# A fused spectral filter and feed-forward kernel: another order of work in its first 50 microseconds

## The chip, the cores and the metric

The kernel runs on one core of one Trainium2 chip. The metric is the time of one execution on the device, in microseconds (us); the time of a kernel is the median of its runs.

A core has five engines that run side by side, each through its own instructions in order: TensorE (PE in the profile, its weight loads PEld) multiplies matrices into PSUM, VectorE (DVE) and ScalarE (ACT) do elementwise work, GpSimd (POOL) does small work here, SyncE (SP) issues DMAs. An instruction waits at the head of its engine's queue until what it needs is there, and everything behind it on that engine waits too.

## What is computed

```python
xn = layernorm(x)                               # x: 2048 rows (tokens) of 1024
s  = irfft2(rfft2(xn) * (w_r + 1j * w_i))       # spectral filter over both axes
g  = silu(silu(xn @ w1) @ w2)                   # w1: 1024 x 3584, w2: 3584 x 1024
return x + s * g
```

## The kernel before, in words

The rows are cut into four **row blocks** c = 0 to 3 of 512 rows, each of four **row tiles** p of 128 rows. w1 is cut into 28 **weight tiles** f of 128 columns. All large products run with f16 operands that are split into a high and a low part; a product of a row block and a weight tile, `mm1(c, f)` (L449), is 24 matmuls of 128 x 512: eight slices of the inner dimension, by (high, high), (high weight, low row) and (low weight, high row).

**A row tile** is prepared in `ln_gen` (L679): `load_x` issues its DMA (L641), `stats` takes its statistics on VectorE (L685 to L688) and three small operations on GpSimd, `norm` normalises on ScalarE (L693), `trans` turns it with eight transposes on TensorE (L702), `hi` copies the high part out of PSUM on ScalarE (L706), `lo` makes the low part on VectorE (L710). Two PSUM buffers serve these transposes and the first stage of the forward transform (`fa_mat`, L762, its matmuls at L766 to L768). Blocks 2 and 3 go another way, `turned` (L650): normalised and copied on ScalarE (L693 and L671), low part on VectorE (L664), then turned by DMA (L657). Their normalised tiles have two buffers, so the third waits for the first one's low part.

**A weight tile** is prepared in `weights1` (L261): `load` issues its DMA (L271), `maxi` takes each row's largest magnitude on VectorE (L274), `scales(i, k)` sums that over the partitions with a small matmul on TensorE (L258) for k tiles together and makes a power of two and its inverse in four to six short VectorE operations (L279 to L287), `split` writes the high part on ScalarE (L251) and `rest` the low part on VectorE (L254). Raw and split tiles share seven buffers.

**The order of the work** is written out by hand: what the program emits is what each engine executes in order. Background work stands in generators, each a job in a queue: `wq` for w1 and later w2, `bg` for row blocks and then the spectral transforms, `xq` for a scan of w2. `slot(queue)` runs the first job on to its next `yield`. The main loop (L1467) goes through `order`, a list of pairs (c, f): first (0, 0) to (0, 3), then (1, 0) to (1, 3), (0, 4), (0, 5), (1, 4), (1, 5), then block 2. Here the products are called by their place n in that list, the first, the fifth and so on (n = 0, n = 4). After each product from n = 4 on, `after` (L1409) evicts the product before it (ScalarE, L465; where a pair of blocks and tiles is complete, also subtractions and splits for the second matrix product, L494 to L499 and L251/L254), and `work` (L1415) gives `wq` one slot and `bg` up to three, as many as a small reckoning of VectorE's and TensorE's work allows. At the n in `EXTRA` `wq` has a second slot. Where a block begins, `finish(bg, ln[c])` (L1470) first runs its job to the end; since that steps the queue until the job reports its end, it also takes the first step of the next job.

Before, the beginning (L1436 to L1459) loads row tiles 0 to 3, then weight tiles 0 to 3; it runs 35 idle matmuls (`spin`, L1428) and then ten slots of `bg` and `wq` in turn, with 8 or 12 idle matmuls after four of them. Weight tiles 0 and 1 are scaled together, then 2 and 3. The first product runs its 24 matmuls by kind of part, the others by slice. For n < 4 each product is followed by one slot of `wq` and 2, 0, 1 and 1 slots of `bg` (L1503): these carry block 1's preparation, the loads of weight tiles 4 and 5 and the reduce of tile 4.

Of the kernel before, what the change touches and what calls it, by code (L numbers as in the profile page):

```python
# [127 lines left out]
def spectral_ffn(ctx, tc, x, w_r, w_i, w1, w2, ca, kc, ci, tw, pm, out):  # L128
    nc = tc.nc
# [112 lines left out]


    xnT, w1t, h32, w2t = {}, {}, {}, {}
    e1, m1, r1, rs, s1 = (small(k, NFT) for k in ("e1", "m1", "r1", "rs1", "s1"))
    ep, hs = small("ep", NP), small("hs", NP)
    w2m = small("w2m", NFT)
# [13 lines left out]
    def weights1():  # L261
# [35 lines left out]
            w1t[i] = w = new.pop(i)  # L297
            low(w[:, 1], raw.pop(i), rs[:, i:i + 1], w[:, 0])

        for i in range(4):  # L300
            load(i)
        yield 0
        maxi(0)
        yield 0
        maxi(1)
        yield 0
        scales(0, 2)
        yield 0
        split(0)
        yield 0  # L310
        rest(0)
        yield 0
        split(1)
        rest(1)
        maxi(2)
        maxi(3)
        yield 0
        scales(2, 2)
        split(2)
        rest(2)  # L320
        yield 2
        split(3)
        rest(3)
        yield 2
        def ahead(i):

            if i < NFT and i not in raw and i - len(used1) <= 4:
# [118 lines left out]

    done2, ready2, chunks = [0], [-1], [0]

    def mm1(c, f):  # L449
        ps = pf.tile([128, 512], F32, name=f"pa{c}_{f}", tag="ff")  # L450
        w, xt = w1t[f], xnT[c]
        terms = [(d, wh, xh) for wh, xh in ((0, 0), (0, 1), (1, 0)) for d in range(8)]
        if c + f:
            terms.sort(key=lambda k: k[0])
        for n, (d, wh, xh) in enumerate(terms):
            nc.tensor.matmul(ps, w[:, wh, d], xt[:, xh, d], start=(n == 0), stop=(n == 23))  # L456
        if c == 3:
            used1.add(f)
        q, g = f // 2, c // 2

        def evac():
            if (q, g) not in h32:
                h32[q, g] = H["p"].tile([128, 4, 512], F32, name=f"h32_{q}_{g}", tag="h32", bufs=2)
            hq = h32[q, g]
            nc.scalar.activation(hq[:, 2 * (c % 2) + f % 2], ps, AF.Silu, scale=s1[:, f:f + 1])  # L465
            if c % 2 and f % 2:
                return hidden(q, g)

        return evac
# [209 lines left out]
    def ln_gen(c):  # L679
# [30 lines left out]
            nc.vector.tensor_tensor(xnT[c][:, 1, :, sl], pst.pop(p), xnT[c][:, 0, :, sl], op=OP.subtract)  # L710

        new_xnT(c)
        if c == 0:
            for p in range(2):
                stats(p)
                norm[p]()
            trans(0)
            hi(0)
            stats(2)
            norm[2]()  # L720
            trans(1)
            hi(1)
            stats(3)
            norm[3]()
            lo(0)
            yield 0
            trans(2)
            hi(2)
            lo(1)
            yield 0  # L730
            trans(3)
            hi(3)
            lo(2)
            yield 0
            lo(3)
            yield 0
            return
        if c in TURNED:
            yield from turned(c, stats, norm)
            return  # L740
        for i in range(4):
            pair = range(2 * (i % 2), 2 * (i % 2) + 2)
            for p in pair:
                if i < 2:
                    stats(p)
                else:
                    trans(p)
                    if c < 3:
                        load_x(c + 1, p)
            if i < 2:  # L750
                yield 2.5
                for p in pair:
                    norm[p]()
                continue
            for fn in (hi, lo):
                for p in pair:
                    fn(p)
            yield 2.5

    psa, l0 = {}, {}  # L760

# [625 lines left out]
    with tc.manual_schedule():  # L1387
# [48 lines left out]
        nc.scalar.activation(warm, ones[:, 0:1], AF.Silu)  # L1436
        J = {}
        open_fwd()
        for i in range(2):
            load_x(0, i)  # L1440
        nc.sync.dma_start(ident, pm[:, 3])
        for i in range(2, 4):
            load_x(0, i)
        w1j = add(wq, weights1())
        slot(wq)
        ln = [add(bg, ln_gen(0)), None, None, None]
        nc.gpsimd.memset(mhalf, -0.5)
        spin(WARM[0])
        for k, q in enumerate((bg, wq, bg, wq, bg, wq, wq, bg, wq, wq)):
            slot(q)  # L1450
            spin(WARM[1 + k])
        for i in range(4):
            load_x(1, i)
            if i == 1:
                load_fwd()
        for c in range(1, 4):
            ln[c] = add(bg, ln_gen(c))
        for c in range(4):
            add(bg, fd_gen(c))  # L1459

# [1 line left out]
        order += [(2, 0), (2, 1), (2, 2), (3, 0), (3, 1), (2, 3), (3, 2), (3, 3), (2, 4), (2, 5), (3, 4), (3, 5)]  # L1462
        order += [(c, f + i) for f in range(6, NFT - LAST, 2) for c in range(4) for i in range(2)]
        order += [(2 * g + c, f + i) for g in range(2) for f in range(NFT - LAST, NFT, 2) for c in range(2) for i in range(2)]
        last_use = {c: max(n for n, k in enumerate(order) if k[0] == c) for c in range(4)}
        left, f_job = len(order), None
        for n, (c, f) in enumerate(order):  # L1467
            left -= 1
            if f == 0 and c:
                finish(bg, ln[c])  # L1470
            if ln[3].done and n >= 22 and not f_job:
                add(xq, wmax_gen())
                max_job = add(xq, w2max_gen())
                f_job = add(bg, switch(A, open_f, 1, max_job))
                add(bg, f_gen())
                add(bg, edge_gen())
                add(bg, switch(B, open_i, 6, lag=2))
                for k in IORDER:
                    add(bg, i_gen(k))
            if left == 2 * LAST + 3:  # L1480
                finish(wq, w1j)
                finish(xq, max_job)
                finish(bg, f_job)
                w2_scales()
                add(wq, w2_gen())
            chunks[0] = sum(last_use[k] < n for k in range(4))
            if left == 3:
                load_h(0, 0, 0, nc.sync)
                load_h(0, 0, 1, nc.sync)
                load_h(0, 1, 0, nc.sync)  # L1490
            if left == 1:
                load_h(0, 1, 1, nc.sync)
            hold[0] = left < 4
            while f not in w1t:
                slot(wq)
            if (c, f) in FILL:
                fa_mat(0, FILL.index((c, f)))
                fa_evac(0, FILL.index((c, f)))
            ev = mm1(c, f)
            if left == 0:  # L1500
                for j, k in ((2, 0), (2, 1), (3, 0)):
                    load_h(0, j, k, nc.sync)
            if n < 4:  # L1503
                slot(wq)
                for _ in range((2, 0, 1, 1)[f]):
                    slot(bg)
                settle()
                fresh_ev[0] = ev
                tick()
                continue  # L1510
# [80 lines left out]
```

## Time and profile before

| | before |
|---|---|
| median of 3 runs | 1243.97 us (1243.03 to 1247.36) |
| profiled execution | 1243.22 us |
| its span, first to last instruction | 1241.4 us |
| TensorE busy | 1222.8 us, 98% |
| VectorE busy | 998.9 us, 80% |
| ScalarE busy | 467.6 us, 38% |
| GpSimd busy | 116.0 us, 9% |

The profile is of one execution. Its busy times are sums over the whole span, and a busy TensorE includes the idle matmuls. The timeline gives each instruction's start and duration from the span's start; where equal instructions follow each other they are merged, with their count. The waits give, for an engine and line, whom it waited for. The granted clock is the share of TensorE's full clock that the chip granted in a stretch.

### The profile page before, as it was taken

The numbers are of one execution on the slowest core, as the hardware profiler recorded it, in microseconds if no ns is written. First come the engines' busy times: TensorE is split into PE (matmuls) and PEld (weight loads), VectorE is DVE, ScalarE is ACT, GpSimd is POOL, SyncE is SP. The second block draws the span as 40 slices with busy tenths as digits, with TensorE's granted clock in tenths as the row PEclk, the third lists the DMA queues.
The fourth block names the chain that finished last, engine by engine and source line by source line (L and its number), as shares of the span: only waits on it lengthen the run. The fifth ranks groups of instructions, "written<-read, shape, count | busy, mean of one in ns | idle before, by whom it ended". The sixth has DMA issues, their size and how long they took to land.

```text
span 1241.4 us, 19019 instructions
## 1 busy us (share of the span) xinstructions
PE 1222.8 (98%) x6991; PEld 626.4 (50%) x6991; DVE 998.9 (80%) x1968; ACT 467.6 (38%) x612; POOL 116.0 (9%) x241
## 2 busy tenths in 40 slices
PE   8999999999999999999999999999999998999997
PEld 5545445444544454445445555544555553555544
DVE  7687988899788898886969899794377785796785
ACT  4865344334554565435433221122132221342211
POOL 1330000001000000010001121114111110000000
PEclk9999999999999999999999999999999999999999
DMA  7487476646668897769899999997989999696897
GB/s 249 135 173 184 134 227 204 186 141 174 207 186 244 271 280 240 221 186 268 187 290 237 304 253 209 273 256 225 270 210 306 261 350 351 227 366 213 267 351 280
DMA packets 272542, 297.87 MB, mean 240 GB/s; under 512 B 40256, under 2 KB 198720, under 8 KB 272064
## 3 DMA queue, kind: packets, MB, share of 16 engines
q1 hardware_dynamic: 252576, 237.85, 65.6%
q10 hardware_dynamic: 15840, 51.45, 12.2%
q0 software_dynamic: 4032, 7.34, 3.4%
q8 instruction: 55, 0.90, 0.3%
q14 instruction: 39, 0.32, 0.1%
HBM read 188.05 MB, written 104.35 MB: 236 GB/s over the span
## 4 chain that ended last, share of the span: by engine, by line
PE 84%; DMA 7%; DVE 6%; ACT 1%; issue 1%; SPq 1%; ACTq 0%; DVEq 0%; POOLq 0%
PE pa L456 46%; PE pb L536 10%; PE pb L535 10%; PE pb L534 10%; PE fx L938 2%; DMA sd<-s 2%; DMA out_dram<-pl 1%; DMA kk<-in_kc_dram 1%; PE iu L1189 1%; PE id L1271 1%; DMA fx<-in_A_x_dram 1%; PE fx L940 1%; PE fx L939 1%; DMA fs<-sd 1%; DMA jr<-in_B_w_dram 1%
## 5 line engine op out<-in xcount | busy, mean ns | idle before, releaser
L456 PE MATMUL pa<-xnT,w 128*128 128x512 f16 x2688 | 585.2, 379 | 1.1 <-ACT w L251 0.7
L456 PEld LDWEIGHTS <-w 128*128 128x128 f16 x2688 | 261.9, 98 | 311.9 <-DVE w L254 1.3
L534 PE MATMUL pb<-w,ht 128*128 128x512 f16 (+1 forms) x798 | 299.5, 375 | 0.0
L536 PE MATMUL pb<-w,ht 128*128 128x512 f16 (+1 forms) x798 | 299.5, 375 | 0.0
L535 PE MATMUL pb<-w,ht 128*128 128x512 f16 (+1 forms) x798 | 299.5, 375 | 0.0
L536 PEld LDWEIGHTS <-ht 128*128 128x128 f16 x798 | 78.1, 98 | 91.1
L534 PEld LDWEIGHTS <-ht 128*128 128x128 f16 x798 | 78.1, 98 | 87.0
L535 PEld LDWEIGHTS <-ht 128*128 128x128 f16 x798 | 78.1, 98 | 87.1
L465 ACT ACTIVATE h<-pa,s 128x512 f32<-128x512 f32 x112 | 75.6, 678 | 120.5 <-PE pa L456 108.6
L251 ACT ACTIVATE w<-jr,sc 128x512 f16<-128x512 f32 x98 | 68.3, 714 | 91.1 <-DMA jr<-in_B_w_dram 37.2
L254 DVE SCALAR_TENSOR_TENSOR w<-jr,sc,w 128x512 f16<-128x512 f32 x98 | 71.2, 744 | 8.1 <-ACT w L251 8.1
L254 DVE SCALAR_TENSOR_TENSOR hoone<-h,hs,hoone 128x2048 f16<-128x2048 f32 x28 | 65.7, 2346 | 8.4 <-ACT hoone L251 8.4
L251 ACT ACTIVATE hoone<-h,hs 128x2048 f16<-128x2048 f32 x28 | 56.0, 1998 | 37.9 <-DVE h L499 26.2
L251 ACT ACTIVATE hosum<-hr,hs 128x1536 f16<-128x1536 f32 x28 | 44.1, 1574 | 66.5 <-DVE hr L495 27.9
L965 ACT ACTIVATE zq<-Z,zs 128x1024 f16<-128x1024 f32 x16 | 18.4, 1149 | 98.5 <-DVE Z L1039 53.8
L254 DVE SCALAR_TENSOR_TENSOR hosum<-hr,hs,hosum 128x1536 f16<-128x1536 f32 x28 | 50.7, 1812 | 3.7 <-DMA hd_one<-hoone 2.6
L494 DVE TENSOR_TENSOR hr<-h 128x1024 f32<-128x1024 f32 x28 | 34.2, 1221 | 23.9 <-ACT h L465 23.8
L251 ACT ACTIVATE w<-w1r,rs 128x1024 f16<-128x1024 f32 x28 | 32.0, 1145 | 46.7 <-DVE w L254 31.8
L274 DVE TENSOR_REDUCE m<-w1r 128x1 f32<-128x1024 f32 x28 | 33.8, 1211 | 16.9 <-DMA w1r<-in_B_w_dram 16.9
L938 PE MATMUL fx<-vq,kq 128*128 128x256 f16 x192 | 43.2, 272 | 0.0
L939 PE MATMUL fx<-vq,kq 128*128 128x128 f16 x192 | 42.0, 219 | 0.0
L940 PE MATMUL fx<-vq,kq 128*128 128x128 f16 x192 | 42.0, 219 | 0.0
(210 smaller groups left out, 1502.9 us busy)
## 6 DMA issues: line engine op xcount, KB each, us to landing
w1r<-in_B_w_dram SPq DMA_DIRECT2D x28, 512.0 KB, 6.4
hd_sum<-hosum SPq DMA_DIRECT2D x56, 256.0 KB, 2.9
hd_one<-hoone SPq DMA_DIRECT2D x56, 256.0 KB, 3.6
hd_dif<-hoone SPq DMA_DIRECT2D x56, 256.0 KB, 3.2
w2m<-in_B_w_dram SPq DMA_DIRECT2D x28, 512.0 KB, 5.1
ht<-hd_dif ACTq DMA_DIRECT2D x32, 448.0 KB, 6.2
jr<-in_B_w_dram SPq DMA_DIRECT2D x56, 256.0 KB, 6.9
ht<-hd_sum ACTq DMA_DIRECT2D x32, 448.0 KB, 6.6
```

Source lines behind the costliest of these rows:

```text
L251: nc.scalar.activation(hi, raw, AF.Copy, scale=scale)
L254: nc.vector.scalar_tensor_tensor(lo, raw, scale, hi, op0=OP.mult, op1=OP.subtract)
L274: nc.vector.tensor_reduce(m1[:, i:i + 1], raw[i], axis=AX.XY, op=OP.max, apply_absolute_value=True)
L456: nc.tensor.matmul(ps, w[:, wh, d], xt[:, xh, d], start=(n == 0), stop=(n == 23))
L465: nc.scalar.activation(hq[:, 2 * (c % 2) + f % 2], ps, AF.Silu, scale=s1[:, f:f + 1])
L494: tt(sums[:, 0:2], hq[:, 0::2], hq[:, 1::2], op=OP.subtract)
L534: nc.tensor.matmul(ps, hh[:, 0], w[:, 0], start=first, stop=False)
L535: nc.tensor.matmul(ps, hh[:, 0], w[:, 1], start=False, stop=False)
L536: nc.tensor.matmul(ps, hh[:, 1], w[:, 0], start=False, stop=last)
L938: nc.tensor.matmul(o, k[:, c, kh, 1], v[:, c, vh], start=(n == 0), stop=False)
L939: nc.tensor.matmul(ps[:, c, 0], k[:, c, kh, 2], v[:, c, vh, 128:256], start=False, stop=False)
L940: nc.tensor.matmul(ps[:, c, 1], k[:, c, kh, 0], v[:, c, vh, 0:128], start=False, stop=(n == 2))
```

## The change

The beginning is written out anew, up to and with the first four products.

- Loads: row tiles 0 and 1, weight tile 0, row tiles 2 and 3, weight tiles 1 to 3. Block 1's four tiles are loaded inside the first product, the constants of the forward transform (L638) after it, weight tiles 4 and 5 after the third.
- Of the idle matmuls only the first 35 stay.
- Every one of the first four weight tiles is scaled alone. Tile 0's reduce and column sum come ahead of the first transposes. Tile 1's scale stands inside the first product, tile 2's inside the second, tile 3's inside the third.
- The first product runs in twelve pieces of eight matmuls, each for a quarter of the rows (128 columns) and one kind of part, in an order by row tile; row tiles 2 and 3 are transposed between pieces. Products 2 to 4 run by kind of part, in three pieces of eight 512-wide matmuls, with evictions and other work between the pieces.
- Block 1's tiles are prepared around products 2 to 4: statistics of tile 0 in product 2, of tile 1 in product 3 behind the scale and split of weight tile 3; the transposes of tiles 0 and 1 before product 4, those of tiles 2 and 3 after it.
- The main loop starts at n = 4. `wq` then stands before the reduce of weight tile 4, and `bg` at the first step of block 2. The check at a block's beginning is left out for block 1.

The core of the diff:

```diff
-WARM = [35, 8, 0, 8, 0, 8, 12, 0, 0, 0, 0]
+WARM = 35
...
-    def mm1(c, f):
+    def mm1(c, f, piece=None):
...
+        if piece:
+            for n, (wh, xh, cols) in enumerate(piece):
+                if callable(wh):
+                    wh()
+                    continue
+                for d in range(8):
+                    nc.tensor.matmul(
+                        ps[:, cols], w[:, wh, d], xt[:, xh, d, cols], start=(n + d == 0), stop=(n == len(piece) - 1 and d == 7),
+                        skip_group_check=True)
...
+        load_x(0, 0)
+        load_x(0, 1)
+        nc.sync.dma_start(ident, pm[:, 3])
+        W["load"](0)
+        load_x(0, 2)
+        load_x(0, 3)
+        for i in range(1, 4):
+            W["load"](i)
         nc.gpsimd.memset(mhalf, -0.5)
...
+        spin(WARM)
+        stats(0)
+        stats(1)
+        norm[0]()
+        norm[1]()
+        W["maxi"](0)
+        W["scales"](0, 1)
+        trans(0)
+        trans(1)
+        stats(2)
+        hi(0)
+        W["split"](0)
+        hi(1)
+        norm[2]()
+        lo(0)
+        stats(3)
+        W["rest"](0)
+        lo(1)
+        norm[3]()
+        W["maxi"](1)
...
+        def third():
+            trans(2)
+            hi(2)
+            for i in range(2):
+                load_x(1, i)
+
+        def fourth():
+            trans(3)
+            hi(3)
+            lo(2)
+            load_x(1, 2)
+            load_x(1, 3)
+
+        def second_scale():
+            W["scales"](1, 1)
+            W["split"](1)
+            lo(3)
+            W["rest"](1)
+            W["maxi"](2)
+
+        ev = mm1(0, 0, [
+            (0, 0, cols[0]), (0, 1, cols[0]), (0, 0, cols[1]), act(third), (1, 0, cols[0]), (1, 0, cols[1]), (0, 1, cols[1]),
+            act(fourth), (0, 0, cols[2]), (1, 0, cols[2]), act(second_scale), (0, 0, cols[3]), (1, 0, cols[3]), (0, 1, cols[2]), (0, 1, cols[3])])
+        load_fwd()
...
+        evs.append(mm1(0, 1, [
+            (0, 0, whole), act(settled), scale_of(2), act(lambda: W["maxi"](3), lambda: stats1(0)), (0, 1, whole), (1, 0, whole)]))
+
+        def begin():
+            stats1(1)
+            norm1[0]()
+            norm1[1]()
+
+        evs.append(mm1(0, 2, [(0, 0, whole), act(settled), scale_of(3), act(begin), (0, 1, whole), (1, 0, whole)]))
+        for i in range(4, 6):
+            W["load"](i)
+        trans1(0)
+        hi1(0)
+        stats1(2)
+        stats1(3)
+        trans1(1)
+        hi1(1)
+        lo1(0)
+
+        def rest_of():
+            norm1[2]()
+            norm1[3]()
+            lo1(1)
+
+        evs.append(mm1(0, 3, [(0, 0, whole), act(settled), act(rest_of), (0, 1, whole), (1, 0, whole)]))
+        for i in range(2, 4):
+            trans1(i)
+            hi1(i)
+            load_x(2, i - 2)
+        settled()
+        lo1(2)
+        lo1(3)
+        for i in range(2, 4):
+            load_x(2, i)
...
         for n, (c, f) in enumerate(order):
             left -= 1
-            if f == 0 and c:
+            if n < 4:
+                continue
+            if f == 0 and c > 1:
                 finish(bg, ln[c])
```

`settled` evicts the product before; `scale_of(i)` is the scale, the split and the low part of weight tile i; `cols` are the quarters and `whole` all 512 columns; `stats1`, `norm1`, `trans1`, `hi1` and `lo1` are block 1's.

More of the change, by code (lines that the diff above doesn't have):

```diff
@@ L298, in rest @@
             low(w[:, 1], raw.pop(i), rs[:, i:i + 1], w[:, 0])
-        for i in range(4):
-            load(i)
+        W.update(load=load, maxi=maxi, scales=scales, split=split, rest=rest)
         yield 0
[L303 to L324, printed above, removed]
         def ahead(i):
@@ L740, in ln_gen @@
             return
[L741 to L758, printed above, removed]
+        N[c] = (stats, norm, trans, hi, lo)
     psa, l0 = {}, {}
@@ L1438, in spectral_ffn @@
         open_fwd()
[L1439 to L1443, printed above, removed]
         w1j = add(wq, weights1())
         slot(wq)
[L1446 to L1455, printed above, removed]
@@ new lines, in spectral_ffn, with act, run @@
+        stats(1)
[16 more added lines that the diff above has]
+        W["maxi"](1)
+        cols = [slice(128 * i, 128 * i + 128) for i in range(4)]
+        whole = slice(0, 512)
+        def act(*fns):
+            def run():
+                for fn in fns:
+                    fn()
+            return run, None, None
@@ new lines, in spectral_ffn, with scale_of, run, settled @@
+        load_fwd()
+        def scale_of(i):
+            def run():
+                W["scales"](i, 1)
+                W["split"](i)
+                W["rest"](i)
+            return act(run)
+        evs = [ev]
+        def settled():
+            evs.pop(0)()
+        evs.append(mm1(0, 1, [
[4 more added lines that the diff above has]
+            norm1[1]()
@@ L1458, in spectral_ffn @@
+        settled()
[3 more added lines that the diff above has]
+            load_x(2, i)
+        ln = [None, None] + [add(bg, ln_gen(c)) for c in range(2, 4)]
         for c in range(4):
```

48 lines of the change are left out of this document (8 added, 40 removed).

## The prediction

> **What bounds the kernel now.** I read the page first, then the waits of TensorE, then the timeline of the first 75 us engine by engine.
>
> ```profile
> span 1241.4 us, 19019 instructions
> ```
>
> ```profile
> PE iu L1189 <- DVE zt L1167: 4.4, 1, 4.4
> PE tp L702 <- ACT x L693: 3.3, 3, 2.2
> PE fa L766 <- DVE xnT L710: 1.5, 1, 1.5
> ...
> PE pa L456 <- DVE w L254: 0.4, 1, 0.4
> ```
>
> The second fence (engine and line, whom it waited for, us in total, times, longest) is nearly the whole list: after its first matmul of w1, TensorE waits 1.5 us once, about 1 us once, and then not before line 1189, deep in the inverse transform. So a microsecond that TensorE gains or loses at the beginning is one of the whole time, unless that late wait takes it up. The question is when the first matmuls run, and when TensorE is free of the beginning for good.
>
> The timeline of the beginning (start, us, engine, line, tile, count; in brackets the idle time before and what ended it), one fence for each engine, first VectorE and ScalarE:
>
> ```profile
> 9.10 0.69 DVE L685 BATCH_NORM_STATS2 st<-x 128x6 f32<-128x512 f32 x1 [1.44 <-DMA x<-in_A_x_dram]
> ...
> 10.55 0.65 DVE L685 BATCH_NORM_STATS2 st<-x 128x6 f32<-128x512 f32 x1
> ...
> 13.03 1.21 DVE L274 TENSOR_REDUCE m<-w1r 128x1 f32<-128x1024 f32 x1
> 14.16 1.21 DVE L710 TENSOR_TENSOR xnT<-tp,xnT 128x1024 f16<-128x1024 f32 x1
> 15.29 1.21 DVE L274 TENSOR_REDUCE m<-w1r 128x1 f32<-128x1024 f32 x1
> ...
> 19.66 2.48 DVE L254 SCALAR_TENSOR_TENSOR w<-w1r,rs,w 128x1024 f16<-128x1024 f32 x2
> ...
> 25.19 0.16 DVE L279 TENSOR_SCALAR e<-s 128x2 int32<-128x2 int32 x1 [0.80 <-PE s L258]
> ...
> 44.48 2.36 DVE L710 TENSOR_TENSOR xnT<-tp,xnT 128x1024 f16<-128x1024 f32 x2 [2.11 <-ACT xnT L706]
> ```
>
> ```profile
> 10.12 1.02 ACT L706 ACTIVATE xnT<-tp 128x1024 f16<-128x1024 f32 x1
> 11.94 1.24 ACT L693 ACTIVATE x<-x,v 128x1024 f32<-128x1024 f32 x1 [0.79 <-POOL v L692]
> ...
> 18.48 2.19 ACT L251 ACTIVATE w<-w1r,rs 128x1024 f16<-128x1024 f32 x2 [0.77 <-DVE rs L282]
> 25.99 1.15 ACT L251 ACTIVATE w<-w1r,rs 128x1024 f16<-128x1024 f32 x1 [5.32 <-DVE rs L282]
> ```
>
> ```profile
> 0.99 5.76 PE L1433 MATMUL spin<-ones 128*128 128x256 f16 x35 [0.99 <-POOL mhalf L1447]
> 8.93 1.16 PE L702 MATMUL tp<-ident,x 128*128 128x128 f32 x8 [2.18 <-ACT x L693]
> ...
> 19.68 5.35 PE L456 MATMUL pa<-xnT,w 128*128 128x512 f16 x24 [0.71 <-ACT w L251]
> ...
> 35.37 1.94 PE L702 MATMUL tp<-ident,x 128*128 128x128 f32 x16
> ...
> 45.75 0.22 PE L766 MATMUL fa<-cas,xnT 128*128 128x128 f16 x1 [1.47 <-DVE xnT L710]
> ...
> 47.09 10.52 PE L456 MATMUL pa<-xnT,w 128*128 128x512 f16 x48
> ```
>
> ```profile
> 101.21 5.18 PE pa L456 x24
> ```
>
> The last row, of the chain, is one product of 24 matmuls: 5.18 us. The first product starts at 19.68, the fifth, of row block 1, at 47.09. That second time is the gauge of the beginning.
>
> **The change part by part.** Steps I use, each from start to start in those rows: statistics of a row tile 1.45 (9.10 to 10.55), reduce 1.13 (13.03 to 14.16), low part of a row tile 1.13 (14.16 to 15.29), low part of a weight tile 1.2 (2.48 for two), statistics to normalising 2.84 (9.10 to 11.94), transposes 0.97 (1.94 for two tiles), transposes to the high copy 1.19 (8.93 to 10.12), reduce to the scale's first operation 0.80 (the idle time at 25.19), from there to the split on ScalarE 0.80 (25.19 to 25.99), split to low part 1.18 (18.48 to 19.66).
>
> *The first tile.* It now takes the third place in SP's queue, which landed at 9.10. Bounds are 9.1 and 10.5 (the fourth place was in use at 10.55); I take 9.6, near the first, since the bytes ahead are the same and this tile's rows are shorter. The two row tiles behind it land by 13.0 at the latest, where the reduce of a tile in the fifth place began. The first is wanted at 12.4, so that may cost 0.6 at worst; the second is wanted at 16. Reduce from 9.6 to 10.8, scale begun 11.6, split possible 12.4. But the column sum now stands ahead of the first transposes on TensorE, which were possible at 8.93: they start at about 11.6. At full clock the high copy would begin at 12.8.
>
> *The clock.* Thirty-six idle matmuls go, so TensorE has nothing from 6.75 until the column sum near 11.2, over 4 us. The trace has one such gap:
>
> ```profile
> 1054.33 6.65 PE L1189 MATMUL iu<-kk,zt 128*128 128x129 f16 x72 [4.42 <-DVE zt L1167]
> ```
>
> ```profile
> 1056.00:1058.00 2.00, 2.00 (x22) 2.00 (x20) 0.16 (x1) 0.60 (x1) 0.00 (x0) 0.50 1.03 380
> ```
>
> After 4.42 us of idling the granted clock (third figure from the end) is 0.50. So I let the eight transposes take twice 0.97: high copy at 13.8, its end and the low part on VectorE at 14.85. Bounds: 1.0 less, or about 1 more if the second eight count too.
> [...]
>
> *The first product in quarters.* 96 matmuls of 128 columns do what 24 of 512 did; I cost that at nothing, since line 766's matmuls of 128 columns also keep pace (24 between 45.75 and 47.09, 1.34 us, so 5.4 for 96). It starts at 14.7 + 1.2 = 15.9, almost 4 us sooner. What then paces it is VectorE, without a gap from 14.85: low part, statistics 15.98, rest of tile 0 17.43, low part 18.63, reduce of tile 1 19.76, low part 20.89. The fourth row tile is normalised from 15.98 + 2.84 = 18.82 to 20.06, its transposes run to 21.3, two pieces of 0.45 to 22.2, then the sum of tile 1, whose scale begins on VectorE at 22.7.
>
> *Scales one at a time.* Four scalings of one tile replace two of two tiles, each with its reduce, its 0.80 there and 0.80 on, and each now inside the work that VectorE is late with: low part 23.6 (after 0.9 of scale), rest 1 24.73, reduce 2 25.93 to 27.1, scale 27.9, split 28.7, rest 2 29.88, reduce 3 31.08, statistics of block 1's first tile 32.21, scale 33.66, split 34.46, rest 3 35.64, statistics of its second tile 36.84, normalised 39.68 to 40.92. VectorE idles 0.8 + 1.1 + 1.1 in this, and before it 1.9 for the first tile (idle since 9.10 - 1.44).
>
> *What waits.* Both transposes of block 1's first tiles stand ahead of the fourth product on TensorE's queue. The third product is done at about 36.5; TensorE then waits some 3 us, with the fourth product behind the transposes, until 40.95. From there: transposes 0.97, product 5.18 to 47.1, transposes and high copy 1.19 to 48.3, then 1.06 to the low part and 1.27 to line 766 (in before high copy about 43.42, low part 44.48, 45.75), so 50.6, and 1.34 more: the fifth product starts at **52.0**, against 47.09. Bringing the start forward 4 us is given back and **4.9 us** are lost.
>
> *Queues one step behind.* Formerly the slots for n < 4 emitted the reduce of tile 4, and closing block 1 pulled the first statistics of block 2 ahead of the fifth product. Now both queues begin empty at n = 4. The rows of before behind it:
>
> ```profile
> 49.72 2.19 ACT L693 ACTIVATE xp<-x,v 128x1024 f32<-128x1024 f32 x1 [0.76 <-POOL v L692]
> ...
> 52.90 2.17 ACT L693 ACTIVATE xp<-x,v 128x1024 f32<-128x1024 f32 x1
> ```
>
> ```profile
> 63.63 1.23 DVE L494 TENSOR_TENSOR hr<-h 128x1024 f32<-128x1024 f32 x1 [4.96 <-ACT h L465]
> 64.77 0.68 DVE L495 TENSOR_TENSOR hr<-h 128x512 f32<-128x512 f32 x1
> 65.37 2.35 DVE L664 TENSOR_TENSOR xs<-xp,xs 128x1024 f16<-128x1024 f32 x2
> 67.64 1.28 DVE L254 SCALAR_TENSOR_TENSOR w<-w1r,rs,w 128x1024 f16<-128x1024 f32 x1
> ```
>
> ```profile
> 70.01 1.56 ACT L251 ACTIVATE hosum<-hr,hs 128x1536 f16<-128x1536 f32 x1
> 71.48 0.66 ACT L465 ACTIVATE h<-pa,s 128x512 f32<-128x512 f32 x1
> 72.05 1.99 ACT L251 ACTIVATE hoone<-h,hs 128x2048 f16<-128x2048 f32 x1
> ```
>
> ```profile
> 68.98 30.90 PE L456 MATMUL pa<-xnT,w 128*128 128x512 f16 x142 [0.44 <-DVE w L254]
> ```
>
> Call the fifth product's start T. Normalising and copying a row tile of block 2 take ScalarE 3.18 (49.72 to 52.90). Formerly two pairs ran from T + 2.6. Now they are emitted after the fifth product's eviction: eviction at T + 5.3, pairs to T + 12.2, next eviction to T + 12.9, two subtractions on VectorE 1.74 to T + 14.6. The sum of tiles 4 and 5 now stands behind the seventh product on TensorE (formerly before it): T + 15.6, scale done T + 16.9. Only then comes the first low part of block 2 (1.2), which frees the buffer that the third pair needs: pairs from T + 18.1 to T + 24.4, split of tile 4, its low part T + 25.6 to T + 26.85. So the ninth product, the first with tile 4, starts at T + 26.9 and not T + 21.9 (68.98 - 47.09); TensorE, free at T + 21.1, waits almost 6 us. The low part of tile 5 is emitted one product later, behind the subtractions of the next eviction; ScalarE does 1.56, 0.66, 1.15 (split 5), 1.99 and 0.66 from T + 25.5 to T + 31.5, VectorE 1.74 to T + 33.2 and the low part 1.28. The tenth product starts at T + 34.5 instead of T + 27.1 (68.98 + 5.18 - 47.09). **7.4 us** more. A drop of the clock in the 6 us wait is hidden behind tile 5.
>
> *At nothing:* the constants of line 638 load later, but are wanted at 50; loads of tiles 4 and 5 and of block 2 stand in SP's queue in the order in which their buffers come free, and are wanted at T or later; the evictions inside the products find ScalarE idle. If block 2's loads came late, that would add to the same ScalarE chain, up to 1 us.
>
> **Sum.** 4.9 + 7.4 = 12.3 on the profiled execution's 1243.22 (span 1241.4 and 1.8 around it; the median of the runs is 1243.97): **1255.5 us**.
>
> **Rivals.**
> *It works* (faster): TensorE never waits after its first piece. Without the clock's drop 14.7 + four products 20.7 + six sets of transposes 5.8 + three sums, each within the 0.80, 1.1 + line 766's 1.34 = 43.6, which is 3.5 before 47.09, and no new wait later: 1239.7. It decides at the transposes of block 1's second tile, which TensorE would reach at 34: the chain on VectorE must be 7 us shorter than I have it. For it: the quarters and the earlier split are real. Against: VectorE's row is full.
> *Only the early loss:* ScalarE catches up and tiles 4 and 5 come as before: 1248.1. *Only the late one:* the early part gains 2.0 (line 766's wait of 1.5 stays): 1243.2 + 5.4 = 1248.6.
> *The loss is taken up:* the wait at line 1189 hangs on a transfer that doesn't move, and its 4.4 us vanish; with the early loss alone 1243.7, no difference.
> *The clock again:* it also drops in the 3 us before block 1's second tile, and the fourth product runs at half for a while; 72 matmuls took 6.65 after the gap at 1049.9, where line 766's pace gives 4.0, so 2.6 more: 1258.1, and to 1261 with the second transposes and a late third block.
>
> **How the numbers follow.** Forecast 0.47; early loss alone 0.10; late loss alone 0.08; clock again 0.11; taken up 0.12; works 0.12. Slower by over 0.3% (3.7 us, about what a measurement can tell from no change, so beyond 1247.7) are the first four: 0.76. Same is 0.12, faster 0.12. The range leaves out only the last rival and the far end of the clock's: 1243 to 1261.
>
> **What would show it.** First w1 matmul near 15.9 (14.7 without the clock's drop); TensorE waiting about 3 us for ScalarE's normalising of block 1's second tile; the fifth product at 52; then waits of some 6 and 2 us on line 254's low parts of tiles 4 and 5, with ScalarE full between. It is wrong if VectorE gets through the first 40 us with clearly less idle time, or if ScalarE's pairs for block 2 start before the fifth product's eviction.

## The result, and the profile after

| | before | after |
|---|---|---|
| median | 1243.5 us (1240.58 to 1247.36, 6 runs) | 1262.06 us (1260.91 to 1267.49, 6 runs) |
| ratio, 95% interval | | 1.0154 [1.0136, 1.0171] |
| profiled execution | 1243.22 us | 1261.47 us |
| VectorE, ScalarE busy | 998.9, 467.6 us | 999.8, 468.2 us |

The changed kernel is 18.6 us slower. No engine has noticeably more work (VectorE 0.9 us, ScalarE 0.6 us); the first line of its page gives the span, 17.9 us longer:

```profile
span 1259.3 us, 19113 instructions
```

TensorE's waits in the changed kernel (whom it waited for, us in total, times, longest):

```profile
PE pa L442 <- ACT w L252: 4.4, 1, 4.4
PE tp L688 <- ACT x L679: 4.1, 3, 3.2
PE s L259 <- DVE m L275: 3.7, 1, 3.7
PE pa L442 <- ACT L L719: 3.1, 1, 3.1
PE iu L1133 <- DVE zt L1111: 2.6, 1, 2.6
...
PE pa L442 <- DVE w L255: 1.3, 2, 0.7
```

Lines have new numbers here: products are L437 (the first four) and L442, weight splits L252 and L255, column sum L259, transposes L688, normalising L679, ScalarE's copy of a turned tile L657, the DMA transposes L643. L1133 was L1189. Against the list of before there are new entries for the column sum, the ninth product (first line) and, later, `ACT L L719`; the longest wait for a tile's normalising (second line) is 3.2 us instead of 2.2. Where they stand, from TensorE's timeline:

```profile
10.35 0.38 PE L259 MATMUL s<-m,ones 128*128 128x1 f32 x2 [3.74 <-DVE m L275]
10.59 3.21 PE L688 MATMUL tp<-ident,x 128*128 128x128 f32 x16
14.24 1.66 PE L437 MATMUL pa<-xnT,w 128*128 128x128 f16 x24 [0.44 <-ACT w L252]
...
39.69 1.97 PE L688 MATMUL tp<-ident,x 128*128 128x128 f32 x8 [3.16 <-ACT x L679]
41.46 7.25 PE L437 MATMUL pa<-xnT,w 128*128 128x512 f16 x24
...
53.30 15.70 PE L442 MATMUL pa<-xnT,w 128*128 128x512 f16 x72
...
78.76 0.60 PE L442 MATMUL pa<-xnT,w 128*128 128x512 f16 x2 [4.44 <-ACT w L252]
80.08 6.70 PE L442 MATMUL pa<-xnT,w 128*128 128x512 f16 x24 [0.72 <-DVE w L255]
87.36 30.82 PE L442 MATMUL pa<-xnT,w 128*128 128x512 f16 x142 [0.58 <-DVE w L255]
...
124.01 0.59 PE L442 MATMUL pa<-xnT,w 128*128 128x512 f16 x1 [3.15 <-ACT L L719]
125.08 13.03 PE L442 MATMUL pa<-xnT,w 128*128 128x512 f16 x47 [0.49 <-DMA xnT<-xs]
```

Before, the sixteenth product, the first of row block 3, came straight behind other matmuls:

```profile
107.57 5.34 PE L456 MATMUL pa<-xnT,w 128*128 128x512 f16 x24
```

The differences of these starts say where the time went (for the tenth product, the start of its third matmul, the first that needs the weight tile's low part):

| start of | before | after | later by | new here |
|---|---|---|---|---|
| first product | 19.68 | 14.24 | -5.4 | |
| fifth | 47.09 | 53.30 | 6.2 | 6.2 |
| tenth | 74.16 (68.98 + 5.18) | 87.36 | 13.2 | 7.0 |
| sixteenth, second matmul | 107.8 | 125.08 | 17.3 | 4.1 |
| first matmul of L938, now L882 | 577.2 | 597.2 | 20.0 | 2.7 |
| first of L1189, now L1133 | 1054.3 | 1072.5 | 18.2 | -1.8 |

The second matmul of before's sixteenth product is taken 0.2 behind its first (5.18 over 24). The 2.7 behind it is the granted clock: 47 matmuls took 13.03 where 47 of those 0.216 make 10.1. The granted clock is the third figure from the end of the windows' rows:

```profile
36.00:40.00 4.00, 0.84 (x7) 0.65 (x7) 3.62 (x9) 1.60 (x2) 2.02 (x6) 0.81 0.39 131
40.00:44.00 4.00, 4.00 (x14) 2.28 (x13) 2.45 (x2) 2.85 (x4) 1.05 (x4) 0.50 0.30 94
44.00:48.00 4.00, 4.00 (x17) 1.72 (x16) 0.00 (x0) 1.56 (x2) 0.00 (x0) 0.84 0.10 39
...
122.00:125.00 3.00, 0.59 (x1) 0.10 (x1) 2.90 (x8) 2.38 (x4) 0.00 (x0) 0.80 1.15 255
125.00:128.00 3.00, 2.92 (x7) 1.05 (x8) 3.00 (x7) 0.00 (x0) 0.11 (x1) 0.50 0.74 210
```

Both of these waits of 3 us are followed by half the clock, the first for some 6.8 us (what is missing in the three rows, 0.19, 0.50 and 0.16 of 4 us, doubled): the fourth product took 7.25 (5.34 in before), the 47 matmuls from the sixteenth product on lost 2.7.

Why the sixteenth waits is read on ScalarE and SP. The first fence is before's normalising of block 3 and its DMA transposes (there L657), the second the same in the changed kernel (start, us, engine, line, tile, count; SPq is the DMA queue of SP):

```profile
82.54 2.16 ACT L693 ACTIVATE xp<-x,v 128x1024 f32<-128x1024 f32 x1
...
88.86 1.99 ACT L251 ACTIVATE hoone<-h,hs 128x2048 f16<-128x2048 f32 x1
...
88.04 6.51 SPq L657 DMA_TRANSPOSE xnT<-xs  x4
...
97.69 5.92 SPq L657 DMA_TRANSPOSE xnT<-xs  x4
```

```profile
99.15 2.00 ACT L252 ACTIVATE hoone<-h,hs 128x2048 f16<-128x2048 f32 x1 [5.86 <-DMA hd_one<-hoone]
...
101.63 2.17 ACT L679 ACTIVATE xp<-x,v 128x1024 f32<-128x1024 f32 x1
...
106.28 16.82 SPq L643 DMA_TRANSPOSE xnT<-xs  x8
```

In before block 3's first normalising stood ahead of the `hoone` copy, now it stands behind it, and that copy waits 5.86 us for a DMA. The normalising begins 48.3 behind the fifth product (101.63 - 53.30) instead of 35.5 (82.54 - 47.09), and the eight transposes run until 123.1. So the wait belongs to them, though its first part is booked on an eviction.

### The profile page after: what moved, and what is told of

It reads as the page before. It is cut to its first block, busy times and chain, and to the rows that moved or that the text cites. A ratio compares the mean times of both kernels' runs of the same rounds, so it can differ in the third digit from the quotient of the medians.

```text
span 1259.3 us, 19113 instructions
## 1 busy us (share of the span) xinstructions
PE 1228.5 (98%) x7031; PEld 629.1 (50%) x7031; DVE 999.8 (79%) x1976; ACT 468.2 (37%) x612; POOL 113.7 (9%) x243
## 4 chain that ended last, share of the span: by engine, by line
PE 84%; DMA 6%; DVE 5%; ACT 3%; issue 1%; SPq 1%; POOL 0%; ACTq 0%; DVEq 0%; POOLq 0%
PE pa L442 41%; PE pb L520 11%; PE pb L521 11%; PE pb L522 11%; DMA jr<-in_B_w_dram 2%; PE fx L882 2%; PE id L1215 1%; DMA pd<-pl 1%; ACT xp L679 1%; DMA out_dram<-pl 1%; PE fx L884 1%; PE fx L883 1%; PE pa L437 1%; PE iu L1133 1%; DMA fs<-sd 1%
## 5 line engine op out<-in xcount | busy, mean ns | idle before, releaser
L442 PE MATMUL pa<-xnT,w 128*128 128x512 f16 x2592 | 568.5, 381 | 9.4 <-ACT w L252 4.4
L442 PEld LDWEIGHTS <-w 128*128 128x128 f16 x2592 | 253.7, 99 | 313.3 <-issue 9.7
L252 ACT ACTIVATE w<-jr,sc 128x512 f16<-128x512 f32 x98 | 68.3, 714 | 90.1 <-DMA jr<-in_B_w_dram 28.9
L255 DVE SCALAR_TENSOR_TENSOR w<-jr,sc,w 128x512 f16<-128x512 f32 x98 | 71.2, 744 | 9.6 <-ACT w L252 9.6
L252 ACT ACTIVATE hoone<-h,hs 128x2048 f16<-128x2048 f32 x28 | 56.0, 1999 | 48.3 <-DVE h L485 20.7
L255 DVE SCALAR_TENSOR_TENSOR hoone<-h,hs,hoone 128x2048 f16<-128x2048 f32 x28 | 65.6, 2344 | 10.1 <-ACT hoone L252 10.1
L252 ACT ACTIVATE hosum<-hr,hs 128x1536 f16<-128x1536 f32 x28 | 44.1, 1574 | 65.8 <-DVE hr L481 35.2
L255 DVE SCALAR_TENSOR_TENSOR hosum<-hr,hs,hosum 128x1536 f16<-128x1536 f32 x28 | 50.7, 1811 | 1.9 <-ACT hosum L252 1.9
L252 ACT ACTIVATE w<-w1r,rs 128x1024 f16<-128x1024 f32 x28 | 32.1, 1146 | 37.2 <-DVE w L255 22.8
L882 PE MATMUL fx<-vq,kq 128*128 128x256 f16 x192 | 43.2, 273 | 0.0
```

The costliest lines, as they stand in the source:

```text
L252: nc.scalar.activation(hi, raw, AF.Copy, scale=scale)
L255: nc.vector.scalar_tensor_tensor(lo, raw, scale, hi, op0=OP.mult, op1=OP.subtract)
L882: nc.tensor.matmul(o, k[:, c, kh, 1], v[:, c, vh], start=(n == 0), stop=False)
```

## The experiments

Each time is a median of several runs, beside runs of the kernel before on the same chip. Two questions were open: which of the early and the late part costs what, and what holds block 3 back.

**One step of each queue put back.** The change, and ahead of the main loop:

```diff
+        slot(wq)
+        slot(bg)
```

> The changed kernel, with one slot of wq (the reduce of weight tile 4) and one of bg (block 2's first statistics) emitted before the fifth product, so that both queues stand there as in the kernel before. Theory (three waits, of which two come from the queues standing one step behind): the fifth product stays at about 53, the ninth and tenth come 22 and 27 us after it, the sixteenth no longer waits for block 3; 6 us slower than before, about 1249.5 us. Rival (the loss is the clock, halved because the idle matmuls are gone): the early gaps stay as they are, so most of the loss stays, 1257 to 1262. Rival (all of it is lost before the fifth product and only handed on): no change, 1262.

Measured: 1258.19 against 1242.78, ratio 1.0109 [1.0078, 1.0139]: a miss of 8.7 us. The ninth product has no wait left, as expected, but the sixteenth has:

```profile
62.44 46.78 PE L442 MATMUL pa<-xnT,w 128*128 128x512 f16 x216
...
116.69 0.58 PE L442 MATMUL pa<-xnT,w 128*128 128x512 f16 x1 [4.79 <-DMA xnT<-xs]
117.88 12.28 PE L442 MATMUL pa<-xnT,w 128*128 128x512 f16 x47 [0.60 <-DMA xnT<-xs]
```

My theory, that the two empty queues are the whole late loss, fell. The single steps show why.

**Only `wq`'s step.**

> The changed kernel with only the slot of wq (reduce of weight tile 4) ahead of the fifth product. Theory: the sum of tiles 4 and 5 comes before the seventh product again and the split of tile 4 ahead of block 2's third normalising, so the 7 us of waiting at the ninth and tenth products go; block 2 and 3 stay one step behind, so the wait at the sixteenth stays, perhaps longer since TensorE comes earlier (4 to 7 us with the clock): 1254 to 1258 us. If what counts is ScalarE's chain of block 2 and not the place of the sum, the ninth product still waits and it stays near 1262.

Measured: 1256.7, ratio 1.011 [1.008, 1.0139]. The time is as expected, the place of the remaining wait is not: the waits for tile 4 are gone, and of 5.1 us of waits for transposes 4.0 (3.46 and 0.58) stand at the thirteenth product, the first of block 2, and 1.1 at the sixteenth, where I had expected the whole.

**Only `bg`'s step.**

> The changed kernel with only the slot of bg (block 2's first statistics) ahead of the fifth product. Theory: ScalarE normalises block 2 from the fifth product on, tile 4's low part is ready before the ninth product needs it, tile 5's about 2 to 3 us late, block 3 in time for the sixteenth: 1250 to 1254 us. If the place of the sum of tiles 4 and 5 is what counts, the ninth and tenth wait as in the changed kernel, and it stays at 1256 to 1262.

Measured: 1264.32, ratio 1.0166 [1.0139, 1.0193]: a miss, no gain at all. Its ninth and sixteenth products stand where the changed kernel has them:

```profile
78.60 1.03 PE L442 MATMUL pa<-xnT,w 128*128 128x512 f16 x2 [4.43 <-ACT w L252]
...
124.08 0.38 PE L442 MATMUL pa<-xnT,w 128*128 128x512 f16 x1 [3.07 <-ACT L L719]
```

Something takes `bg`'s step back. It is the small reckoning. It books every matmul on TensorE, the idle ones too: 36 of them, 256 columns at 0.4215e-3, make 3.9 us. With these gone it stands, when the fifth product has been emitted, at 34.4 for TensorE and, with `bg`'s step put back, at 37.2 for VectorE (38.4 with both steps), and `work` gives `bg` no slot while VectorE is more than 1.0 ahead. A step put back by hand is then withheld behind the fifth product. (Without it, in the changed kernel, VectorE stands at 34.3 and `bg` has its slot: there the empty queue is enough to make block 3 late.)

**The reckoning put back as well.** Both steps, and

```diff
+        clock["pe"] += 36 * 256 * 0.4215e-3
```

> The change, with one step of wq and one of bg put back before the fifth product, and with the 3.9 us of the 36 removed idle matmuls (256 columns each) added to the reckoning's account of TensorE. VectorE's and ScalarE's instructions then stand in the order of before from the beginning's end on; only the beginning itself is the change's. Theory (two things push the queues back: the empty start and the reckoning; the waits of the ninth, tenth and sixteenth products all come of that): the fifth product at 52 to 53.3, the ninth product 22 us after it without a wait of over 0.7 us, the sixteenth without a wait for its transposes, and only the early loss left: 1248 to 1250. Rival (the sixteenth product waits because everything before it is late, not because of the order): it still waits some 4 us, as with the two steps alone, and the time is 1255 to 1258.

Measured: 1249.22 against 1243.43, ratio 1.0059 [1.0037, 1.0081]. The fifth product is at 52.56, and the sixteenth waits no more:

```profile
75.60 30.89 PE L442 MATMUL pa<-xnT,w 128*128 128x512 f16 x142 [1.58 <-DVE w L255]
...
107.67 5.34 PE L442 MATMUL pa<-xnT,w 128*128 128x512 f16 x24
```

(The second row is the fifteenth; the sixteenth follows it without idle time.) With the steps back, one figure in a reckoning that no engine executes is worth 9.6 us in the medians here (15.4 lost with the steps alone, 5.8 with the figure, each against its own runs of before). In the two profiled executions the first matmul of the forward transform comes 5.4 sooner (583.8 instead of 589.2); the rest lies behind that point, where the edge stage's clock fell in the first of the two executions (0.54 between 859 and 861) and not in the second (1.00 from 849 to 860; last section). The ninth product waits 1.58 where I had said at most 0.7.

**The reckoning alone, in the kernel of before.** If this is right, it must slow the old kernel too:

```diff
+            if n == 4:
+                clock["pe"] -= 36 * 256 * 0.4215e-3
```

> The kernel of before, and one figure in its reckoning: ahead of the fifth product 3.9 us are taken off TensorE's account, what the 36 removed idle matmuls stood for. No instruction is added or removed; from the fifth product on some of VectorE's and ScalarE's work is issued one product later. Theory (the reckoning alone holds block 3 back, and TensorE then waits for its transposes): the fifth product at 47.1 and the ninth near 69 as in before, the sixteenth with a wait of 3 to 5 us for the transposes and half the clock after it, as in the run with the two steps alone: 1249 to 1253. Rival (the order matters only because the change is late everywhere): no new wait of over 1 us, 1242 to 1245.

Measured: 1251.13 against 1242.89, ratio 1.0072 [1.0051, 1.0093], as expected: 8.2 us. The account stands at 34.4 for TensorE and 37.5 for VectorE behind the fifth product, and `bg`'s slot is withheld; in before it is 38.3 and 37.5, and it is given. The same instructions on the same engines, in another order, and the wait of the sixteenth product is there:

```profile
111.56 0.58 PE L456 MATMUL pa<-xnT,w 128*128 128x512 f16 x1 [4.87 <-ACT h L465]
112.79 12.58 PE L456 MATMUL pa<-xnT,w 128*128 128x512 f16 x47 [0.65 <-DMA xnT<-xs]
```

The first matmul's wait is booked on an eviction, the 47 others wait for the transposes. The fifth product is at 46.73, so nothing is late before it; the first matmul of the forward transform is (584.5 instead of 577.2). This shows, without the changed beginning, that one step of `bg` makes block 3 late. The rival, that the order only matters when everything is late, is out.

**The early part: the transposes moved.** The change, with the transposes of block 1's second tile behind two thirds of the fourth product:

```diff
-        trans1(1)
-        hi1(1)
         lo1(0)
         def rest_of():
+            trans1(1)
+            hi1(1)
...
-        evs.append(mm1(0, 3, [(0, 0, whole), act(settled), act(rest_of), (0, 1, whole), (1, 0, whole)]))
+        evs.append(mm1(0, 3, [(0, 0, whole), act(settled), (0, 1, whole), act(rest_of), (1, 0, whole)]))
```

> The changed kernel with the transposes of block 1's second tile moved from ahead of the fourth product to before its last third. Theory: the wait of 3.2 us for the normalising is covered by two thirds of the product, the clock isn't halved there, the fifth product starts near 48.5 and not 53.3; the waits at the ninth, tenth and sixteenth, which hang on the fifth, stay: about 1257 us. Rival (ScalarE or VectorE, not the order on TensorE, sets the fifth product): no gain, 1261 to 1262.

Measured: 1260.61, ratio 1.0141 [1.0109, 1.0174]: a miss of 3.6 us. The early half was right: the fifth product starts at 48.29, 5.0 sooner than in the changed kernel, the tenth and sixteenth come 5.0 and 4.9 sooner, the last matmul of L882 still 5.1 (835.6 instead of 840.7). The whole gained only about 1. In the profiled execution 3.5 of the 5.1 are lost at the small matmuls of the edge stage (L1013 to L1015), where the clock fell, and the rest at the late wait of L1133 (4.0 instead of 2.6):

```profile
861.00:863.00 2.00, 1.91 (x14) 1.42 (x14) 0.72 (x3) 1.60 (x2) 0.89 (x6) 0.89 0.03 8
863.00:865.00 2.00, 2.00 (x6) 0.70 (x5) 2.00 (x3) 0.87 (x3) 1.62 (x5) 0.50 0.70 199
```

**Steps, reckoning and moved transposes together.**

> The same, and besides the transposes of block 1's second tile moved behind two thirds of the fourth product. Theory (the early loss is TensorE's wait at those transposes and the clock that it costs): fifth product near 48.3, which is 1.2 later than in before, no later wait that before does not have: 1244 to 1246. Rival (what is gained early is given back at the edge stage and the late inverse transform, as in the run with the move alone): 1247 to 1249.

Measured: 1246.1 against 1243.43, ratio 1.0024 [1.0007, 1.004], 0.1 us above what was expected. The wait and the half clock are gone from the fourth product (1.00 from 36 to 48), and the fifth is 4.5 sooner than without the move (52.56):

```profile
39.82 1.05 PE L688 MATMUL tp<-ident,x 128*128 128x128 f32 x8
40.70 1.89 PE L437 MATMUL pa<-xnT,w 128*128 128x512 f16 x8
...
48.09 10.52 PE L442 MATMUL pa<-xnT,w 128*128 128x512 f16 x48
```

So the move is worth 3.1 us in the medians (1249.22 - 1246.1, both beside the same runs of before).

**The clock by itself.** The change with 32 more idle matmuls at the start and 27 ahead of the transposes at 39.69:

```diff
-        spin(WARM)
+        spin(WARM + 32)
...
         hi1(0)
+        spin(27)
```

> The change, with 32 more idle matmuls at the start and 27 ahead of the transposes of block 1's second tile, so that TensorE is busy in its two idle gaps and the granted clock has no reason to fall; the order of all else is as it was. Theory (the clock is the smaller part of the loss): the first high copy about 1 us sooner if the clock stays up, the fourth product at full speed, so the fifth at 50 to 51 instead of 53.3, everything behind it as before relative to it: 1258 to 1260. Rival (the clock is the main loss): 1255 or less. Rival (idle matmuls stand in the way of the sum or of the transposes): 1262 or more.

Measured: 1257.11 against 1243.43, ratio 1.0118 [1.0089, 1.0147], 5 us less than the change, 0.9 more than expected. The granted clock stays at 1.00 from 8 to 16 and from 32 to 48, the fourth product takes 5.34, the fifth starts at 49.77, 3.5 sooner. The wait of the ninth stays (4.44), and the sixteenth still waits, 1.35 and 0.71 us for its transposes:

```profile
118.69 0.38 PE L442 MATMUL pa<-xnT,w 128*128 128x512 f16 x1 [1.35 <-DMA xnT<-xs]
```

The clock is the smaller part, 3.5 us at the fifth product. Another 1.8 comes from that shorter wait (the sixteenth's second matmul is 70.0 behind the fifth product instead of 71.8), and 1.7 is lost again further on, at a wait for an eviction; the forward transform's first matmul comes 4.5 sooner (592.7 instead of 597.2). The 59 idle matmuls are booked as well, 6.4 us. Yet `work` gives `bg` the same slots behind every product as in the change, and block 3's normalising still stands behind the `hoone` copy (96.94 and 94.46). So the booking without `bg`'s step does not help either: each of the two alone makes block 3 late, and both have to be put back.

**Quarters alone.** The kernel of before, its first product in quarters:

> The kernel of before, its first product by quarters of the tokens (96 matmuls of 128 columns instead of 24 of 512), in the same place and without the other work between them. Theory (quarters cost nothing): the first product takes 5.2 to 5.6 us and the fifth starts at 47.1 to 47.4; 1243 to 1244.5. Rival (each quarter matmul has a fixed cost that the change hid in its waits): first product 7 us or more, 1245 or more.

Measured: 1244.56 against 1242.89, ratio 1.0017 [1.0, 1.0034]. The product's two stretches:

```profile
19.13 1.07 PE L458 MATMUL pa<-xnT,w 128*128 128x128 f16 x16 [0.71 <-ACT w L251]
20.45 4.64 PE L458 MATMUL pa<-xnT,w 128*128 128x128 f16 x80 [0.25 <-DVE w L254]
```

5.7 us of matmuls instead of 5.35, the fifth product at 47.20 (47.09), the first matmul of the forward transform at 577.2 in both. That is not yet the price: this execution's first product starts 0.55 earlier (19.13 instead of 19.68). From there to the fifth it takes 28.07 instead of 27.41 in before (27.41 also in the run with the reckoning alone, whose beginning is before's). So quarters cost 0.7 us in this place, of which 0.25 is a wait for the weight tile's low part, which they need sooner. The median is 1.7 higher, and its interval touches 1.

**Can the new beginning win?** Two attempts on top of the run with everything. First, the statistics of block 1's second tile ahead of weight tile 3's split, and the transposes spread between pieces of the fourth product:

```diff
                 W["scales"](i, 1)
+                if i == 3:
+                    stats1(1)
                 W["split"](i)
...
+        evs.append(mm1(0, 3, [
+            (0, 0, whole), act(settled), act(turn1), (0, 1, whole), act(turn2), (1, 0, slice(0, 256)), act(turn3), (1, 0, slice(256, 512))]))
```

> As the run with both steps, the reckoning and the moved transposes, and besides: the statistics of block 1's second tile ahead of the low part of the fourth weight tile, and the transposes of block 1's last three tiles spread between the pieces of the fourth product. Theory (VectorE's order, not its load, holds the norm of that tile back, and 1.9 us of TensorE's waits between 43 and 47 go): fifth product at 46.5 to 47.2, 1242.5 to 1244.5, no difference from before that can be told. Rival (ScalarE, full from 38 to 47, sets that stretch whatever the order): fifth product near 48.3 as without these moves, 1244.5 to 1246.

Measured: 1246.36, ratio 1.0024 [1.001, 1.0038]: 1.9 us above what was expected. The fifth product starts at 45.73, 1.4 ahead of before, so the order did hold it back and not ScalarE's load; how much of it was VectorE's order and how much the spread transposes, made in one edit, is not separated. But the ninth has nothing of it, and pays for its wait with the clock:

```profile
69.13 32.51 PE L442 MATMUL pa<-xnT,w 128*128 128x512 f16 x142 [1.95 <-DVE w L255]
```

```profile
70.00:72.00 2.00, 2.00 (x7) 0.77 (x6) 1.90 (x5) 2.00 (x3) 0.12 (x1) 0.56 1.08 203
```

Block 2's first normalising is at 49.91, against 49.72 in before: VectorE takes its statistics behind a reduce. So second, `slot(bg)` ahead of `slot(wq)`, and 32 more idle matmuls at the start (the figure added to the reckoning falls from 36 matmuls to 4):

> The last kernel of the series before, with bg's step ahead of wq's, so that block 2's first statistics stand before the reduce of the fifth weight tile on VectorE, and with 32 more idle matmuls at the start (the figure in the reckoning lowered by as much). Theory (ScalarE's normalising of block 2 sets the ninth product, and it waits for VectorE's order): ScalarE's first pair of block 2 at 48.8 instead of 49.9, the ninth product at 68.0 instead of 69.1, a wait there of under 1 us and no half clock behind it: 1242 to 1244, no more than 0.1% from before. Rival (block 2's rows land too late for that): first pair at 49.9 as before, 1245 to 1247.

Measured: 1245.13 against 1242.89, ratio 1.0017 [1.0002, 1.0031], 1.1 us above what was expected. The normalising comes at 49.22, the ninth product at 68.44 with a wait of 0.82 and at full pace behind it (30 matmuls in 6.72, 0.22 each), the forward transform's first matmul at 576.6, 0.6 ahead of before. The gain does not reach the end: in the profiled execution the clock fell again at the edge stage (0.50 between 847 and 851). No version here beats the kernel before.

## Why the prediction was wrong in its size

The direction and the two mechanisms it named were right; 6.6 us were missing (18.6 against 12.0 on the medians). On the profiled executions it is 5.9 (18.2 against 12.3): 1.3 at the fifth product, -0.4 at the tenth, 6.8 at the sixteenth, -1.8 at the late wait.

- *First product at 15.9, clock down in the gap:* it started at 14.24. The first tile's reduce began at 9.07 instead of 9.6, and the clock fell in this execution (transposes 3.21 for 16). That gap, 2.3 to 3.7 us in the runs with this beginning, brought the clock down in five of eight executions (after, e1b_wq, e1c_bg, e6_slots_reck, e7_all: 0.50 in a window of 2 us between 10 and 14) and not in three (e1_both, e2_trans, e8_best: 1.00 from 6 to 16). The drop in the sum came from the one gap of 4.42 us; what decides between the five and the three is not shown.
- *Quarters at nothing:* 0.7 us in the kernel of before, measured from the first product to the fifth. In the change VectorE set the pace there, so it is not seen.
- *TensorE waits some 3 us at block 1's second tile:* 3.16, and removing it brought the fifth product forward by 5.0 and 4.5.
- *Fifth product at 52.0, 4.9 lost:* 53.30, 6.2 lost. What failed is that the sum had the clock's second drop only as a rival, with 0.11. It fell after that wait in all five executions that have it. The drop cost 1.9 us on the fourth product and 0.8 on the transposes ahead of it (39.69 to 41.46, where 0.97 was reckoned); the transposes came 1.3 sooner than forecast, and 1.3 more was lost in all.
- *Queues one step behind, 7.4:* 7.0, with the tenth product at T + 34.06 where T + 34.5 was forecast. This was no luck: ScalarE's first pair comes behind the fifth product's eviction (59.27 behind 58.68), its next pairs at T + 18.0 (18.1 forecast), the ninth product's low part at T + 26.8 (26.9). But of that chain `wq`'s step is the cause: put back alone, it removes these waits.
- ***At nothing*: this is the step that failed.** Past the tenth product nothing more was priced, and a late block 3 stood only in the far end of a rival. It cost 4.1 of waiting and 2.7 of half clock. I had followed the empty queues only to the tenth product. `bg`, one step behind, puts block 3's normalising behind the `hoone` copy and its transposes in one row behind that, and this comes due at the sixteenth. The empty queue was enough for that. Besides, the step "Thirty-six idle matmuls go" counted TensorE's clock and missed that they also stood in the account that decides when `bg` has a slot, and this alone is enough, too: it costs 8.2 us in the old beginning. In the changed one only both put back help, 9.6 us over `bg`'s and `wq`'s steps without the figure.
- *The loss taken up at the late wait:* 1.8 us of 20 (its 4.4 became 2.6), not all of it. Nor does that wait hang on something that stays in its place: with both steps put back, 12.0 us late at the forward transform (589.2), it is 5.3. What sets it is not shown.

The medians divide the loss so: 5.8 for the beginning alone, 9.6 for `bg`'s step and the reckoning together, and 3 to 5 for `wq`'s step (18.6 less the 15.4 of the run with both steps, where `bg`'s has no effect without the figure, or less the 13.9 of `wq`'s step alone). These are differences along one row of runs, so that they add up proves nothing by itself.

What stays open is where the last 2 us of the repaired versions go. The edge stage's clock fell only in executions where its small matmuls had gaps between them or before them (below), but what makes the gaps is not shown, and a profile is one execution, while the medians only show the sum.

## What to carry to other kernels

When an edit removes instructions, look for whatever counts them: a planner's account, a slot, a threshold can move work that the edit never touched, and what it moves may come due 65 us later (46.73 to 111.56 in the old beginning). A step said to cost nothing should be followed on each engine to the next point where another block begins, with the copies and DMAs it would then stand behind. And a wait of 3 us on TensorE should be priced with the half clock that may follow it: 1.5 to 2.7 us more beside the 3.16 in the five executions that have that wait.

## What the runs showed of the hardware

- The clock also fell after shorter idling than the 4.42 us of before: after 3.16 us in five of five executions (0.50 to 0.60 between 40 and 44), in one after a single wait of 1.95 us (e8_best, 0.56 between 70 and 72). By the pace of its matmuls it fell after waits of 1.35 and 0.71 us in e4_spin, too: 40 took 10.48 us, where 40 of 0.216 make 8.6. At the start it fell after 2.26 us (e6_slots_reck, 0.50 between 10 and 12) and not after 3.60 (e2_trans, 1.00 from 6 to 16). So in these runs the length of one gap does not decide. Whether the transposes and column sums beside some of these gaps count as work for the clock, no run here separates.
- It fell without a wait of over 1 us, too. The edge stage has 18 f32 matmuls of 128x24 and 128x8. In four of the thirteen profiled executions (before, after, e6_slots_reck, e7_all) they ran without a gap, and the clock held. In the other nine there were gaps between them or before them, and in six of these the clock was near 0.5 for 3 to 7 us (0.50 to 0.54 in the lowest window of 2 us). First before, where they take 1.9 us, then e8_best, where they take 3.0 (the second figure is TensorE's busy time):

```profile
842.00:845.00 3.00, 3.00 (x23) 2.19 (x20) 2.50 (x9) 0.40 (x1) 3.00 (x13) 1.00 0.00 0
845.00:847.00 2.00, 2.00 (x13) 1.21 (x14) 1.22 (x2) 1.86 (x4) 0.51 (x2) 1.00 0.28 30
```

```profile
845.00:847.00 2.00, 1.39 (x9) 0.81 (x7) 2.00 (x7) 0.00 (x0) 2.00 (x7) 1.00 0.00 0
847.00:849.00 2.00, 1.91 (x15) 1.82 (x15) 0.72 (x4) 1.22 (x2) 1.26 (x8) 0.87 0.00 0
849.00:851.00 2.00, 2.00 (x7) 0.62 (x6) 2.00 (x3) 0.67 (x2) 1.25 (x3) 0.50 0.41 66
```

TensorE counts as busy 3.30 of the 4 us up to 849 in e8_best. So in this execution TensorE, mostly busy by the profile, lost its clock (0.50 between 849 and 851) while its matmuls were this small and stood apart; what decides among the nine executions is not shown.
